# First expert's products in 128-token tiles, wider-spaced transposes, and routing constants spread over attention

## The chip, the core and the metric

The kernel runs on one core of a Trainium2 chip. The metric is device time in microseconds (us). It was run three times: 687.61, 686.19 and 683.44 us, median 686.19 us. One further execution was taken with the profiler; it lasted 685.43 us by the same clock, and its span from the first to the last instruction is 683.8 us. All times "at" some moment below are counted from the start of that span.

## What is computed

Sliding-window attention over 8 batches, 8 heads, 576 positions and 64 values a head; its output, seen as 4608 tokens of 512 values, goes through a mixture of 8 experts with a fixed capacity of 576 tokens each.

```python
def _attn_ref(q, k, v):
    scores = matmul(q, k.T) / sqrt(D)
    # a row sees itself and the 63 rows before it
    attn = softmax(where(mask, scores, -1e9))
    return matmul(attn, v)

def _moe_ref(x, w_gate, w1, w2):
    flat = (x @ w_gate).flatten()
    for idx in argsort(-flat):          # the best pairs first
        tok, e = idx // E, idx % E
        if assigned[tok] >= 0 or counts[e] >= N // E: continue
        assigned[tok] = e; counts[e] += 1
    for e in range(E):
        out[assigned == e] = relu(x[assigned == e] @ w1[e]) @ w2[e]
```

Everything is float32. The products of the experts are made exact enough by splitting each operand into a high part in a rounded 32-bit format (names ending in `h`) and a remainder (names ending in `l`), and adding three products: high by high, low by high and high by low.

## The kernel before

**Attention** (`attention`) runs 72 steps, one for 128 query rows and four heads. A step issues the score matmuls (L126), the softmax on VectorE (L135) and ScalarE (L145), the transposes of the weights (L152, evacuated at L154) and the products with V (L173). Nine steps make one batch. Twice in a batch, the gate's logits are computed too (L85 to L112). At the end of every step from the fifth on, three entries of `setup` are issued: this is the generator `Routing.constants`, 64 small operations, three of them on GpSimd and the rest on VectorE, that build tables the routing needs later. Three a step use it up by step 25.

**Routing** (`Routing.steps`) finds, for one expert at a time, the tokens of highest logit, by eight rounds of a 16-way search. Each round compares all logits with 15 thresholds on VectorE (L461), counts with small matmuls (L518 for the first expert, L532 after it) and picks the next digit. It ends with the list of the expert's 576 tokens (`idx`, L692). The routing of expert 0 has nothing beside it; that of every later expert lies beside the products of the expert before.

**Experts** (`Experts`). For each expert:
- `load` fetches eight chunks of weights (four of `w1`, four of `w2`) and splits them: high part by ScalarE (L790), remainder by VectorE (L794, the first three chunks of expert 0) or by ScalarE and an adding transfer from GpSimd's queue (L799, L801). For expert 0, chunks 3 to 7 start only once `turned` says that all transposes are issued.
- `turn` gathers the tokens with five indirect transfers (L844), 128 tokens each and 64 in the last. It transposes each tile on TensorE (L856) into a buffer `tp`, of which there are two, and splits it: `xh` by ScalarE (L832), then `xl` by VectorE (L835).
- `steps` makes the first products (L897): for each of eight blocks `f` of the hidden layer one unit of 12 matmuls over tokens 0 to 255 and one over tokens 256 to 575. The order begins with three units of the first kind. Each unit is evacuated by ScalarE (`hh`, L874) and VectorE (`hl`, L879). Then come the second products: the last 64 tokens (L929), then four tiles of 128 tokens (L939), each 24 matmuls of 512 columns.

**The order on each engine is written by a planner.** `Streams` runs the Python generators by a clock of its own: each generator issues instructions and says how long they should take (`busy`, `yield`), and the generator whose time comes next issues next. The engines then execute in that order, each in its own queue, and wait for the data they need. So a planned time does not delay anything by itself: it decides what stands ahead of what. `GATHER` is the planner's guess of how long the gathered rows take, and `there` the planned moment at which the last tile has come; tile `a` is planned 1040 ns times (4 - a) ahead of it, and never closer than about 900 ns to the tile before. The first 256-column units may be issued when `XT` is set, after the second tile; those of 320 columns when all five tiles are there (`turned`).

```python
there = self.clock() + self.busy(5200, "pool") + GATHER[min(p, 2)]
yield lambda: self.first == p
...
yield max(0, there - 1040 * (4 - a) - self.clock())
...
yield dt + 600
```

The routing of expert 1 is planned from `turned` of expert 0 on, too.

Of the kernel before, what the change touches and what calls it, by code (L numbers as in the profile page):

```python
# [9 lines left out]
FT = mybir.dt.float32  # L10
# [4 lines left out]
AF = mybir.ActivationFunctionType  # L15
# [7 lines left out]
E = 8  # L23
# [7 lines left out]
def attention(ctx, tc, c, q, k, v, vt, gate, xs, L, choices, setup, counters):  # L31

    nc = tc.nc
# [190 lines left out]
    n = len(seq)  # L224
# [17 lines left out]
    last = []  # L242

    def store(m, x):
        nc.sync.dma_start(xs[128 * m:128 * m + 128], x.rearrange("p h d -> p (h d)"))

    for s in range(n + 4):
        old = seq[s - 4] if 4 <= s else None
        if s < n:
            qk(*seq[s], old)  # L250
        else:
            rs, inv, gates, values = norm(*old)

            for f in (rs, inv, values, gates) if s < n + 2 else (rs, inv, gates):
                f()
            if s >= n + 2:
                last.append(values)
            while late:
                late.pop(0)()
        if 1 <= s < n + 1:  # L260
            sm(*seq[s - 1])

        if stores and (len(stores) > HOLD or s > LOADED):
            store(*stores.pop(0))
        if 2 <= s < n + 2:
            tr(*seq[s - 2])
        if 3 <= s < n + 3:
            pv(*seq[s - 3])
        for f, a in at.get(s, []):
            f(*a)  # L270
        if late:
            late.pop(0)()
        if s > 3:
            for _ in range(3):
                next(setup, None)
    for f in last:
        f()
# [61 lines left out]
CAP = NT // E  # L339
# [390 lines left out]
NCH = 4  # L730
NX = DM // 128
NF = F // 128
LAG = 1500
STAGE = 6

GATHER = (2600, 3800, 6200)
SEND = 3400
LOAD = 2600
ADDED = 4500
# [2 lines left out]
class Experts:  # L742
    def __init__(self, ctx, tc, c, xs, w1, w2, out, ring=8):
        self.tc, self.nc, self.c = tc, tc.nc, c
        self.xs, self.w1, self.w2, self.out = xs, w1, w2, out
        self.ring = ring
        self.fw = ctx.enter_context(tc.tile_pool(name="fw", bufs=1))
        self.ps = ctx.enter_context(tc.tile_pool(name="fp", bufs=1, space=PSUM))
        self.W = {}
        self.XT = {}  # L750
        self.used = 0
        self.taken = 0
        self.first = 0
        self.gathered = 0
        self.sent = 0
        self.turned = 0

    def room(self):
        return self.ps.tile([128, 320], FT, name="h", bufs=3)
# [64 lines left out]
    def turn(self, p, idx):  # L824

        nc, fw = self.nc, self.fw
        yield lambda: self.turned == p

        def evac(a, n, t):
            r = slice(128 * a, 128 * a + n)  # L830
            t = t.bitcast(FT)
            nc.scalar.activation(xh[:, :, r], t[:, :, :n], AF.Copy)  # L832
            yield 700
            self.busy(600, "dve")
            nc.vector.tensor_tensor(xl[:, :, r], t[:, :, :n], xh[:, :, r].bitcast(FT), OP.subtract)  # L835

        def half():
            self.XT[p] = (xh, xl)
            yield 0

        g = fw.tile([128, 5, DM], FT, name="xg")
        for a in range(5):
            n = 128 if a < 4 else 64
            nc.gpsimd.indirect_dma_start(out=g[0:n, a], out_offset=None, in_=self.xs,  # L844
                                         in_offset=IndirectOffsetOnAxis(ap=idx[0:n, a:a + 1], axis=0))
        self.gathered += 1
        there = self.clock() + self.busy(5200, "pool") + GATHER[min(p, 2)]
        yield lambda: self.first == p
        xh = fw.tile([128, NX, CAP], FR, name="xh")
        xl = fw.tile([128, NX, CAP], FR, name="xl")  # L850
        for a in range(5):
            n = 128 if a < 4 else 64
            yield max(0, there - 1040 * (4 - a) - self.clock())
            t = self.ps.tile([128, NX, 128], FR, name="tp", bufs=2)
            for cc in range(NX):
                nc.tensor.transpose(t[:, cc, :n], g[0:n, a, 128 * cc:128 * cc + 128].bitcast(FR), self.c["identr"][0:n, 0:n])  # L856
            dt = self.busy(300)
            self.spawn(evac(a, n, t), dt + 150)
            yield dt + 600
            if a == 1:  # L860
                self.spawn(half(), 600)
        yield 1500
        self.turned += 1

    def steps(self, p, idx):
        nc, fw = self.nc, self.fw
        xh, xl = self.XT[p]

        hh = fw.tile([128, NF, CAP + 64], FR, name="hh")
        hl = fw.tile([128, NF, 512], FR, name="hl")  # L870

        def evac(f, n, h):
            w = h.shape[1]
            nc.scalar.activation(hh[:, f, 256 * n:256 * n + w], h, AF.Relu)  # L874
            yield 500
            for c, m, t in ((0, 256, hl[:, f, 256 * n:256 * n + 256]), (256, 64, hh[:, f, CAP:])):
                if c < w:
                    self.busy(m + 79, "dve")
                    nc.vector.scalar_tensor_tensor(t, h[:, c:c + m], 0.0,  # L879
                                                   hh[:, f, 256 * n + c:256 * n + c + m].bitcast(FT),  # L880
                                                   op0=OP.max, op1=OP.subtract)

        order = [(f, n) for f in range(NF) for n in range(2)]

        order[:6] = [(f, n) for n in range(2) for f in range(3)]
        for f, n in order:
            yield lambda: (p, f // 2) in self.W
            if n:
                yield lambda: self.turned > p
            wh, wl = self.W[p, f // 2]  # L890
            r = (slice(0, 256), slice(256, CAP))[n]
            h = self.room()[:, 0:r.stop - r.start]
            k = 0
            for wt, xt in ((wh, xh), (wl, xh), (wh, xl)):
                wv = wt.rearrange("p (c f) -> p c f", c=NX)
                for cc in range(NX):
                    nc.tensor.matmul(h, wv[:, cc, 128 * (f % 2):128 * (f % 2) + 128], xt[:, cc, r],  # L897
                                     start=(k == 0), stop=(k == 11))
                    k += 1
                    if k % 3 == 0:  # L900
                        yield self.busy((360, 441)[n])
            self.spawn(evac(f, n, h), 100)
            if f % 2 and n:
                self.spawn(self.free(1), LAG)
        self.first += 1

        def put(a, o):
            ot = fw.tile([128, DM], FT, name="ot", bufs=3)
            m = 128 if a < 4 else 64
            if a < 4:  # L910
                nc.scalar.activation(ot, o, AF.Copy)  # L911
            else:
                t = fw.tile([64, DM], FT, name="low")
                nc.scalar.activation(t, o[64:128], AF.Copy)
                yield 650
                self.busy(600, "dve")
                nc.vector.tensor_tensor(ot[0:64], o[0:64], t, OP.add)
            yield max(600, self.sent + SEND - self.clock())
            nc.gpsimd.indirect_dma_start(out=self.out,  # L919
                                         out_offset=IndirectOffsetOnAxis(ap=idx[0:m, a:a + 1], axis=0),  # L920
                                         in_=ot[0:m], in_offset=None)
            self.sent = self.clock() + self.busy(1040, "pool")


        o = self.ps.tile([128, DM], FT, name="o", bufs=2)
        for f in range(NF):
            yield lambda: (p, NCH + f // 2) in self.W
            for n, w in enumerate(self.W[p, NCH + f // 2]):
                nc.tensor.matmul(o, hh[:, f, 512:], w[:, 512 * (f % 2):512 * (f % 2) + 512],  # L929
                                 start=(f == 0 and n == 0), stop=(f == NF - 1 and n == 1))  # L930
                yield self.busy(228)
        self.spawn(put(4, o), 100)
        for a in range(4):
            o = self.ps.tile([128, DM], FT, name="o", bufs=2)
            k = 0
            for f in range(NF):
                wh, wl = self.W[p, NCH + f // 2]
                for wt, ht in ((wh, hh), (wl, hh), (wh, hl)):
                    nc.tensor.matmul(o, ht[:, f, 128 * a:128 * a + 128], wt[:, 512 * (f % 2):512 * (f % 2) + 512],  # L939
                                     start=(k == 0), stop=(k == 23))  # L940
                    k += 1
                    yield self.busy(228)
            self.spawn(put(a, o), 100)
        self.spawn(self.free(NCH), LAG)
# [95 lines left out]
```

## Time and profile before

| quantity | value |
|---|---|
| median of three runs | 686.19 us |
| profiled execution, its own time | 685.43 us |
| profiled execution, span | 683.8 us |
| mean granted clock of TensorE | 0.969 |
| attention, last evacuation of a transpose | 165.66 us |
| list of expert 0's tokens (L692) | 193.41 us |
| first product of expert 0 (L897) | 201.58 us |
| second products of expert 0 (L929) | 235.06 us |
| first product of expert 1 | 274.31 us |
| first product of expert 7 | 625.39 us |

The profile gives, for each instruction, its engine, line, output and inputs, start and duration. A duration of a matmul is modelled and overlaps the next one, so the pace of a group is the distance between starts. A wait "[1.66 <-DMA xg]" in front of an instruction is the time its engine sat idle before it and what ended that time. "PEclk" is the clock granted to TensorE, as a share of the full one.

### The profile page before, as it was taken

How to read it: one execution, taken by the hardware profiler on the slowest of the kernel's cores; microseconds unless marked ns; L12 is line 12 of the kernel's file. 1: busy time of each engine (PE TensorE's matmuls, PEld its weight loads, DVE VectorE, ACT ScalarE, POOL GpSimd, SP SyncE). 2: the span in 40 equal slices, each digit the busy share in tenths (PEclk: the TensorE clock that was granted, in tenths of full speed). 3: DMA queues.
4: the chain of work that ended last, by engine and by line, in shares of the span. 5: the costliest groups of instructions: out<-in, count | busy, mean ns of one | idle time of the engine just before them, and what ended most of it. 6: DMA issues, size and time to landing. Idle time of an engine off the chain costs nothing. (4 is left out here: it accounts for less than half of the span.)

```text
span 683.8 us, 16913 instructions
## 1 busy us (share of the span) xinstructions
PE 639.7 (94%) x6365; PEld 537.0 (79%) x6365; DVE 454.6 (66%) x2262; ACT 360.5 (53%) x733; POOL 176.3 (26%) x203
## 2 busy tenths in 40 slices
PE   7799999998469998999999999999999999999995
PEld 5566777776449875997897799789779889978984
DVE  5999988988776765895896787687778611220300
ACT  4688888886035435627437165444607715634410
POOL 1321222220041115207125132321512433112011
PEclk9999999999559999999999999999999999999998
DMA  8999978921066549829678767938937993962501
GB/s 291 337 361 369 365 279 307 385 97 69 13 202 150 114 145 260 200 47 307 173 140 285 177 149 251 226 83 224 240 123 156 295 266 104 249 163 75 97 24 46
DMA packets 49682, 134.09 MB, mean 196 GB/s; under 512 B 4672, under 2 KB 10432, under 8 KB 49600
## 3 DMA queue, kind: packets, MB, share of 16 engines
q0 software_dynamic: 15552, 54.01, 34.9%
q1 hardware_dynamic: 34048, 79.00, 32.6%
q8 instruction: 50, 0.82, 0.5%
q14 instruction: 32, 0.26, 0.1%
HBM read 82.13 MB, written 18.87 MB: 148 GB/s over the span
## 5 line engine op out<-in xcount | busy, mean ns | idle before, releaser
L879 DVE SCALAR_TENSOR_TENSOR hl<-h,hh 128x256 fp32r<-128x256 f32 x128 | 53.6, 419 | 94.7 <-ACT hh L874 93.8
L939 PE MATMUL o<-wh,hh 128*128 128x512 f32 x256 | 102.6, 401 | 0.0
L939 PE MATMUL o<-wl,hh 128*128 128x512 f32 x256 | 102.3, 399 | 0.0
L939 PE MATMUL o<-wh,hl 128*128 128x512 f32 x256 | 101.4, 396 | 0.0
L145 ACT ACTIVATE pe<-st,mx 128x128 f32<-128x128 f32 x288 | 91.4, 390 | 10.2 <-DVE mx L135 9.0
L874 ACT ACTIVATE hh<-h 128x256 fp32r<-128x256 f32 (+1 forms) x128 | 52.2, 408 | 83.3 <-PE h L897 82.0
L897 PE MATMUL h<-xh,wh 128*128 128x256 f32 (+1 forms) x512 | 94.2, 303 | 0.0
L897 PE MATMUL h<-xh,wl 128*128 128x256 f32 (+1 forms) x512 | 93.4, 301 | 0.0
L897 PE MATMUL h<-xl,wh 128*128 128x256 f32 (+1 forms) x512 | 91.5, 299 | 0.0
L919 POOL DMA_INDIRECT out<-ot,idx x40 | 41.1, 1028 | 191.6 <-ACT ot L911 48.8
L135 DVE CUSTOM_DVE_ANT_0 st<-Sp,mask 128x128 f32<-128x128 f32 x288 | 78.6, 277 | 15.6 <-PE Sp L126 11.5
L911 ACT ACTIVATE ot<-o 128x512 f32<-128x512 f32 x32 | 19.1, 598 | 127.8 <-PE o L939 122.6
L897 PEld LDWEIGHTS h<-xh,wh 128*128 128x128 f32 x512 | 77.2, 192 | 1.1 <-issue 0.4
L897 PEld LDWEIGHTS h<-xh,wl 128*128 128x128 f32 x512 | 76.6, 192 | 0.1
L897 PEld LDWEIGHTS h<-xl,wh 128*128 128x128 f32 x512 | 76.1, 191 | 0.1
L801 POOL DMA_DIRECT2D wl<-st x61 | 55.2, 1063 | 74.5 <-ACT wl L799 53.6
L844 POOL DMA_INDIRECT xg<-xs,idx x40 | 39.8, 995 | 119.6 <-DMA st<-w 40.6
L790 ACT ACTIVATE wh<-st 128x1024 fp32r<-128x1024 f32 x64 | 67.2, 1051 | 6.4 <-DMA st<-w 6.4
L799 ACT ACTIVATE wl<-wh 128x1024 fp32r<-128x1024 f32 x61 | 64.4, 1056 | 0.5
L939 PEld LDWEIGHTS o<-wh,hh 128*128 128x128 f32 x256 | 48.5, 189 | 9.3
L939 PEld LDWEIGHTS o<-wh,hl 128*128 128x128 f32 x256 | 48.4, 189 | 9.1
L939 PEld LDWEIGHTS o<-wl,hh 128*128 128x128 f32 x256 | 48.6, 190 | 8.7
(175 smaller groups left out, 1137.8 us busy)
## 6 DMA issues: line engine op xcount, KB each, us to landing
wl<-st POOLq DMA_DIRECT2D x61, 512.0 KB, 6.8
st<-w SPq DMA_DIRECT2D x59, 512.0 KB, 7.5
xs<-x SPq DMA_DIRECT2D x36, 256.0 KB, 4.8
VO<-v SPq DMA_DIRECT2D x6, 1168.0 KB, 16.0
VT<-vt SPq DMA_DIRECT2D x6, 1152.0 KB, 10.5
Q<-q SPq DMA_DIRECT2D x6, 1152.0 KB, 12.9
K<-k SPq DMA_DIRECT2D x6, 1152.0 KB, 14.4
st<-w POOLq DMA_DIRECT2D x5, 512.0 KB, 6.0
```

The source lines that it names most:

```text
L135: nc.vector.tensor_tensor_reduce(st[:, h, :], Sp[h % 2][:, h // 2], mk, scale=-0.125, scalar=3.0e38, op0=OP.add, op1=OP.min, accum_out=mx[ ...
L145: nc.scalar.activation(pe[:, h, :], st[:, h, :], AF.Exp, bias=mx[:, h:h + 1], scale=-1.0)
L790: nc.scalar.activation(hi, st[i], AF.Copy)
L799: nc.scalar.activation(lo, hi.bitcast(FT), AF.Copy, scale=-1.0)
L801: nc.gpsimd.dma_start(lo.bitcast(FT), st[i], accum_op=OP.add)
L844: nc.gpsimd.indirect_dma_start(out=g[0:n, a], out_offset=None, in_=self.xs, in_offset=IndirectOffsetOnAxis(ap=idx[0:n, a:a + 1], axis=0))
L874: nc.scalar.activation(hh[:, f, 256 * n:256 * n + w], h, AF.Relu)
L879: nc.vector.scalar_tensor_tensor(t, h[:, c:c + m], 0.0, hh[:, f, 256 * n + c:256 * n + c + m].bitcast(FT), op0=OP.max, op1=OP.subtract)
L897: nc.tensor.matmul(h, wv[:, cc, 128 * (f % 2):128 * (f % 2) + 128], xt[:, cc, r], start=(k == 0), stop=(k == 11))
L911: nc.scalar.activation(ot, o, AF.Copy)
L919: nc.gpsimd.indirect_dma_start(out=self.out, out_offset=IndirectOffsetOnAxis(ap=idx[0:m, a:a + 1], axis=0), in_=ot[0:m], in_offset=None)
L939: nc.tensor.matmul(o, ht[:, f, 128 * a:128 * a + 128], wt[:, 512 * (f % 2):512 * (f % 2) + 512], start=(k == 0), stop=(k == 23))
```

## The change

There are four edits.
1. Attention issues three of the routing's constants a step only up to step 9, and one a step from step 10 on. The 64 entries then last to step 55.
2. In `turn`, the planned length of the five gathers is 6400 ns in place of 5200, `GATHER` is 2900 for expert 0 and 6500 for the others (before: 2600, 3800 for expert 1, 6200 for the rest), the planned distance of tiles is 1280 ns in place of 1040, and after a tile's transposes the generator waits `dt + 1000` in place of `dt + 600` for experts 1 to 7.
3. Readiness of tokens is counted by tile (`tiles`). The products of expert 0 may begin after the first tile, those of the others after the second as before; a unit waits for the tiles it reads.
4. Expert 0's units become: six blocks `f` over tokens 0 to 127, six over 128 to 255, six over 256 to 575, and then blocks 6 and 7 as before. That is 12 units of 128 columns in place of 6 of 256. The other experts keep their units and order. A chunk of weights is released after its last unit, which for expert 0 comes later than before for the early chunks.

```diff
         if s > 3:
-            for _ in range(3):
+            for _ in range(3 if s < 10 else 1):
                 next(setup, None)
...
-GATHER = (2600, 3800, 6200)
+GATHER = (2900, 6500)
...
+        self.tiles = [0] * E
...
             nc.vector.tensor_tensor(xl[:, :, r], t[:, :, :n], xh[:, :, r].bitcast(FT), OP.subtract)
-
-        def half():
-            self.XT[p] = (xh, xl)
-            yield 0
+            self.tiles[p] = a + 1
+            if a == (1 if p else 0):
+                self.XT[p] = (xh, xl)
...
-        there = self.clock() + self.busy(5200, "pool") + GATHER[min(p, 2)]
+        there = self.clock() + self.busy(6400, "pool") + GATHER[p > 0]
...
-            yield max(0, there - 1040 * (4 - a) - self.clock())
+            yield max(0, there - 1280 * (4 - a) - self.clock())
...
-            yield dt + 600
-            if a == 1:
-                self.spawn(half(), 600)
+            yield dt + (1000 if p else 600)
...
-        def evac(f, n, h):
-            w = h.shape[1]
-            nc.scalar.activation(hh[:, f, 256 * n:256 * n + w], h, AF.Relu)
+        def evac(f, c0, h):
+            c1 = c0 + h.shape[1]
+            nc.scalar.activation(hh[:, f, c0:c1], h, AF.Relu)
             yield 500
...
-        order = [(f, n) for f in range(NF) for n in range(2)]
-
-        order[:6] = [(f, n) for n in range(2) for f in range(3)]
-        for f, n in order:
+        if p:
+
+            units = [(f, n) for n in range(2) for f in range(3)] + [(f, n) for f in range(3, NF) for n in range(2)]
+            units = [(f, 256 * n, (256, CAP)[n]) for f, n in units]
+        else:
+
+            units = [(f, *r) for r in ((0, 128), (128, 256), (256, CAP)) for f in range(6)]
+            units += [(f, *r) for f in range(6, NF) for r in ((0, 256), (256, CAP))]
+        last = [max(n for n, u in enumerate(units) if u[0] // 2 == i) for i in range(NCH)]
+        for n, (f, c0, c1) in enumerate(units):
             yield lambda: (p, f // 2) in self.W
-            if n:
-                yield lambda: self.turned > p
+            yield lambda: self.tiles[p] * 128 >= c1
...
-                        yield self.busy((360, 441)[n])
-            self.spawn(evac(f, n, h), 100)
-            if f % 2 and n:
+                        yield self.busy(3 * (13.5 + (c1 - c0) / 2.4))
+            self.spawn(evac(f, c0, h), 100)
+            if n in last:
                 self.spawn(self.free(1), LAG)
```

More of the change, by code (lines that the diff above doesn't have):

```diff
@@ L870, in steps @@
         hl = fw.tile([128, NF, 512], FR, name="hl")
-        def evac(f, n, h):
-            w = h.shape[1]
-            nc.scalar.activation(hh[:, f, 256 * n:256 * n + w], h, AF.Relu)
+        def evac(f, c0, h):
+            c1 = c0 + h.shape[1]
+            nc.scalar.activation(hh[:, f, c0:c1], h, AF.Relu)
             yield 500
[L876 to L880, printed above, removed]
-                                                   op0=OP.max, op1=OP.subtract)
-        order = [(f, n) for f in range(NF) for n in range(2)]
-        order[:6] = [(f, n) for n in range(2) for f in range(3)]
-        for f, n in order:
+            for a, b, t in ((c0, min(c1, 512), hl[:, f, c0:min(c1, 512)]), (512, c1, hh[:, f, CAP:])):
+                if a < b:
+                    self.busy(b - a + 79, "dve")
+                    nc.vector.scalar_tensor_tensor(t, h[:, a - c0:b - c0], 0.0, hh[:, f, a:b].bitcast(FT),
+                                                   op0=OP.max, op1=OP.subtract)
+        if p:
[6 more added lines that the diff above has]
+        for n, (f, c0, c1) in enumerate(units):
             yield lambda: (p, f // 2) in self.W
-            if n:
-                yield lambda: self.turned > p
+            yield lambda: self.tiles[p] * 128 >= c1
             wh, wl = self.W[p, f // 2]
-            r = (slice(0, 256), slice(256, CAP))[n]
-            h = self.room()[:, 0:r.stop - r.start]
+            h = self.room()[:, 0:c1 - c0]
             k = 0
@@ L896, in steps @@
                 for cc in range(NX):
-                    nc.tensor.matmul(h, wv[:, cc, 128 * (f % 2):128 * (f % 2) + 128], xt[:, cc, r],
+                    nc.tensor.matmul(h, wv[:, cc, 128 * (f % 2):128 * (f % 2) + 128], xt[:, cc, c0:c1],
                                      start=(k == 0), stop=(k == 11))
```

## The prediction

> **What bounds the kernel now.** I read the page's shares and slices first, then who TensorE waited for, then the engines' busy time in short stretches, then TensorE's own instructions in order of time.
>
> ```profile
> PE 639.7 (94%) x6365; PEld 537.0 (79%) x6365; DVE 454.6 (66%) x2262; ACT 360.5 (53%) x733; POOL 176.3 (26%) x203
> ...
> PEclk9999999999559999999999999999999999999998
> ...
> L897 PEld LDWEIGHTS h<-xh,wh 128*128 128x128 f32 x512 | 77.2, 192 | 1.1 <-issue 0.4
> ```
>
> Read the share of PE in the first line, and the fives of PEclk: TensorE is busy 94% of the span, and only in slices 11 and 12 (171 to 205 us), where expert 0 is routed, is its clock about half. From there to the end its products follow one another, so what counts is each stretch in which it stands still or is slowed. From 197 us on its waits are these (total us, times, longest):
>
> ```profile
> PE tp L856 <- DVE xl L835: 5.3, 8, 1.0
> PE tp L856 <- DMA xg<-xs,idx: 4.4, 4, 1.7
> ```
>
> So 9.7 us of waits stand in front of transposes: 4.4 for gathered rows, 5.3 for a `tp` buffer whose `xl` VectorE had not yet written. The waits also cost clock. These stretches are 3.41 us long, cut where the granted clock changes (columns: length; busy time of PE, PEld, DVE, ACT and POOL; clock; DMA share, GB/s):
>
> ```profile
> 193.87:197.28 3.41, 3.41 (x15) 1.83 (x13) 2.48 (x4) 2.94 (x3) 2.18 (x3) 0.50 0.53 183
> 197.28:200.69 3.41, 1.09 (x9) 0.78 (x8) 3.31 (x8) 1.19 (x2) 2.80 (x3) 1.00 0.71 173
> 200.69:204.11 3.42, 3.05 (x17) 2.99 (x18) 2.21 (x6) 0.78 (x3) 1.91 (x4) 0.50 0.77 214
> 204.11:207.52 3.41, 3.41 (x18) 3.12 (x18) 1.54 (x3) 1.19 (x3) 0.00 (x0) 0.50 0.90 341
> 207.52:210.93 3.41, 3.41 (x28) 3.41 (x28) 2.13 (x6) 2.51 (x4) 0.00 (x0) 1.00 0.04 14
> ...
> 265.54:268.95 3.41, 1.84 (x12) 1.33 (x13) 2.36 (x5) 2.58 (x6) 1.21 (x2) 1.00 1.03 193
> 268.95:272.37 3.42, 3.42 (x16) 2.52 (x17) 2.02 (x8) 0.38 (x1) 0.69 (x1) 0.50 1.11 165
> ```
>
> A stretch with PE busy 1.09 or 1.84 us is followed by one at 0.50, a full one (193.87, 204.11) by one at 1.00; the 3.05 of 200.69 was not enough. Eight of that stretch's 17 records are the transposes of two tiles, and 8 or 9 are products: at half clock some 0.22 us each (twice the 0.120 found below, less their fixed part), 1.8 in all. In 204.11, 4 of 18 are transposes, and the products fill some 2.6 us. So between 1.8 and 2.6 us of products in a stretch raise the clock. From 197 to 300 us three stretches run at half.
>
> **First expert.** All transposes (ns of one: least, median, most), and TensorE at the junction:
>
> ```profile
> L856 PE MATMUL tp<-identr,xg x160: 222/247/339, 198.0 to 602.7; 128*128 128x128 f32 x128, 64*128 64x64 f32 x32
> ...
> 198.01 0.53 PE L856 MATMUL tp<-identr,xg 128*128 128x128 f32 x4 [0.70 <-DMA xg<-xs,idx]
> ...
> 201.58 0.97 PE L897 MATMUL h<-xh,wh 128*128 128x256 f32 x3
> ...
> 209.07 0.64 PE L897 MATMUL h<-xl,wh 128*128 128x256 f32 x4
> 209.55 0.75 PE L897 MATMUL h<-xh,wh 128*128 128x320 f32 x4
> 210.14 0.75 PE L897 MATMUL h<-xh,wl 128*128 128x320 f32 x4
> ```
>
> Starts four matmuls apart give the pace at full clock: (209.55 - 209.07)/4 = 0.120 us for 256 columns, (210.14 - 209.55)/4 = 0.147 for 320.
>
> *Price of narrow units.* 12 units of 128 columns replace 6 of 256: 144 matmuls for 72. No product of 128 columns is in the trace. The line through 256 and 320 columns gives 0.067 us. The nearest rows are the transposes, 128 columns with a new stationary tile each: the group at 263.01 below takes 0.46 for four, less one median duration of 0.25, over three: 0.071. The group at 198.01, which came to an idle engine, gives 0.094. I take 0.071, since products come one behind another: 144 x 0.071 = 10.2 against 72 x 0.120 = 8.6, +1.6 us (ends +1.0 and +4.9). The evacuations double in number beside TensorE; in the rows above DVE is busy 1.5 to 2.2 and ACT 0.8 to 2.5 of 3.41 us, so they are hidden, and would cost their own time if not.
>
> The Trainium skill, "TensorE: Matmul & The Clock Gate", section "Back-to-back issue gap", puts a stream of weight load and matmul at about 81 ns for 128 columns; by it the sum would be 144 x 0.081 - 8.6 = +3.1 us in place of +1.6. The transposes' 0.071 speaks for less.
>
> *Earlier start.* Tile 0's first products need only its `xh`, so TensorE has work from about 199.6 on, between transposes, in place of 201.58 (198.01 + 0.53, and an estimated 1 us for ScalarE's copy and the second tile, which comes 1.5 us behind the first). By 204.1 some 33 narrow matmuls are done (11 ahead of 200.69, then 3.4 less 1.0 for two tiles' transposes, at 0.11 each: 22), worth 16 wide ones, where 8 wide were: 8 x 0.120 = 1.0 us won. The stretch 200.69 to 204.11 then holds 2.4 us of products in place of 1.8, nearer to the 2.6 that raised the clock. So I take it to rise one stretch earlier: half of the 2.9 us of products there, 1.45 won (ends 0 and 3.1, if the clock never falls). Sum: +1.6 - 1.0 - 1.45 = -0.9.
>
> The Trainium skill, "TensorE: Matmul & The Clock Gate", section "Part 4: PE-mode transpose", says that transposes do not count as activity for the clock in the same way; the row at 200.69 agrees.
>
> *What is late next.* Chunks 3 to 7 wait for `turned`, which the planner now puts 1.5 us later (there: 6400 + 2900 for 5200 + 2600). The last chunk already was just in time:
>
> ```profile
> 235.91 0.85 POOL L801 DMA_DIRECT2D wl<-st  x1 [5.12 <-ACT wl L799]
> ...
> wl<-st POOLq DMA_DIRECT2D x1, 512.0 KB, 4.5
> ...
> 240.24 0.42 PE L532 MATMUL rps<-G,one 128*32 128x60 bf16 x9 [1.12 <-DVE q L599]
> 240.58 0.51 PE L929 MATMUL o<-wl,hh 128*128 128x512 f32 x1
> ```
>
> Issued at 235.91, it landed at 240.4, and the second products went on at 240.58; the wait named as VectorE's is in part this one. ACT splits that chunk behind the evacuations of the first products, so it moves with them, but the planner leaves TensorE 1.5 us less of other work before it. Of the 0.9 won I give 0.6 back: first expert **-0.3** (ends -3.0 and +4.5). The routing of expert 1, planned from `turned`, stands 1.5 us later in the queues of TensorE and VectorE; nobody waits for it but expert 1's gathers. On SP's and POOL's queues nothing is passed: the gathers, loads and adds keep their order.
>
> **Expert 1's transposes.**
>
> ```profile
> 261.88 0.53 PE L856 MATMUL tp<-identr,xg 128*128 128x128 f32 x4 [1.66 <-DMA xg<-xs,idx]
> 263.01 0.46 PE L856 MATMUL tp<-identr,xg 128*128 128x128 f32 x4
> ...
> 266.49 0.54 PE L856 MATMUL tp<-identr,xg 128*128 128x128 f32 x4 [0.96 <-DVE xl L835]
> 268.41 0.50 PE L856 MATMUL tp<-identr,xg 64*128 64x64 f32 x4 [0.62 <-DVE xl L835]
> 274.31 0.64 PE L897 MATMUL h<-xh,wh 128*128 128x256 f32 x4
> ```
>
> TensorE stood from 260.22 on (261.88 less 1.66) until the rows came. The first tile was planned 9000 - 4 x 1040 = 4840 ns after the list; now it is 12900 - 4 x 1280 = 7780, that is 2.9 us or 12 matmuls of L939 later: it meets TensorE at about 263, after the rows. Distances grow from 1.04 to 1.3 or more, which covers waits of 0.96 and 0.62. Idle won: 1.66 + 0.96 + 0.62 = 3.2; and a denser stretch 265.54 should not drop the clock, which saves half of 3.4 = 1.7. Together 4.9; I keep 0.4 of waits, **-4.5** (ends -4.9 and -1.5). The tiles now end at the end of expert 0's second products, about 268.5; expert 1's first units need two tiles, written by some 266.5 to 267, and three units of 12 x 0.120 = 1.4 us cover the last three tiles. Were that cover gone, TensorE would wait for `xl`, some 2 us per tile.
>
> **Experts 2 to 7.** Of the 5.3 us for `xl`, 5.3 - 1.58 = 3.7 lie here, six waits of some 0.6. A pair of tiles now lies about 0.35 x 2 = 0.7 further apart, so most vanish: **-3.0** (ends -3.7 and -1.0). The work itself is unchanged and hides under the second products.
>
> **Attention.** Steps 18 to 22 (edges are the evacuations at L154) beside the same five steps of a later batch, then the gate's steps with three constants in each of the first two, beside the same without:
>
> ```profile
> 51.62:60.89 9.27, 8.18 (x151) 6.13 (x153) 9.08 (x67) 7.35 (x21) 3.35 (x5) 1.00 1.05 357
> 111.72:119.30 7.58, 7.58 (x145) 5.70 (x141) 6.56 (x56) 7.02 (x22) 3.37 (x5) 1.00 1.01 379
> 64.62:74.13 9.51, 9.51 (x169) 6.53 (x169) 9.20 (x66) 7.64 (x22) 1.39 (x2) 1.00 1.01 356
> 104.27:113.75 9.48, 9.48 (x169) 6.50 (x169) 8.86 (x61) 7.64 (x22) 1.76 (x3) 1.00 0.71 232
> ```
>
> In the first pair VectorE is the bound (9.08 of 9.27) and the steps are 1.69 us longer; two thirds of the constants leave: about -1.2. In the second pair constants cost 0.03, so one more a step to step 55 is hidden by VectorE's slack. **-1.2** (ends -1.9 and +1.0; DMA, at 1.05, may hold part back).
>
> **Sum.** -0.3 - 4.5 - 3.0 - 1.2 = -9.0. Against the profiled execution's own 685.43 (span 683.8 and 1.6 around it) that is 676.4; the median of the runs is 0.8 above it, so **677 us**.
>
> **Rivals.**
> 1. *Waits move rather than vanish.* ACT and DVE evacuate tiles behind other work, as the 0.96 us at 266.49 shows; later places can collide anew. With half of 4.5 + 3.0 kept, 677 + 3.75 + 1 = 682. The fixed distances speak against it, the planner's ignorance for it.
> 2. *The junction gains nothing.* The clock stays at 0.50 to 207.52 and narrow matmuls take 0.094: 677 + 1.45 + 3.3 = 682.
> 3. *Constants on the path.* If the gate's steps have no slack for them, 46 x 0.15 us come in place of -1.2: 677 + 8 = 685. The 0.03 speaks against it.
> 4. *Slower: narrow matmuls wait for their weights.* Weight loads show 192 ns on the page. Were they not hidden, 144 x (0.192 - 0.071) = +17: 694. It decides from 0.135 us a matmul on (144 x 0.064 = 9.2, the whole gain). Against it: 256 columns run at 0.120 with the same 192 ns, so loads do overlap.
>
> The Trainium skill, "TensorE: Matmul & The Clock Gate", section "LDWEIGHTS (loading the stationary operand)", gives about 107 ns for 128 columns; laid end to end with the matmul this would be some 12 us more, 689; the pace of 0.120 disagrees.
>
> **How the numbers follow.** Forecast 0.60, first rival 0.20, second 0.09, third 0.05, fourth 0.06. The three middle ones stay within 1% of 686.2 (679.3 to 693.1, about what a measurement can tell from no change) but for a little of the first: faster 0.62, same 0.32, slower 0.06. The low end takes the far ends of three gains (-3.7, -4.9, -1.9) and a junction at -3, 673, less 2 for scatter: 671. The high end reaches past the rivals of 682 to the third: 685.
>
> **What would show it.** First product near 199.5 and twelve units of about 0.85 us; clock 1.00 from about 204; no wait above 0.5 us before L856; none at 0.50 after 260; steps 18 to 22 near 8 us. Wrong would be: narrow paces above 0.09, a longer wait for the last chunk, first products of expert 1 waiting for tiles.

## The result: slower by 2.6%, and the profile after

The changed kernel takes 702.49 us (median of 6 runs, 701.35 to 705.57) against 685.38 us for the kernel before (6 runs, 682.85 to 687.61). The ratio is 1.0257, with a 95% interval from 1.0224 to 1.029. The profiled execution took 701.35 us, its span is 699.7 us. The time of 677 us was missed, and so was the range. In experiment 5 below, two of ten executions were slow (702.84 and 706.73 us, mean clock 0.950 and 0.939; the other eight 0.965 to 0.974, the changed kernel's own 0.940 to 0.951) and are left out of its figures.

From the page of the changed kernel, the shares and the granted clock in 40 slices:

```profile
PE 659.1 (94%) x6437; PEld 558.6 (80%) x6437; DVE 452.0 (65%) x2268; ACT 362.9 (52%) x739; POOL 177.4 (25%) x203
...
PEclk9999999998555799999999999999999999999998
```

TensorE has 72 matmuls more than before and 19.4 us more of busy time. There are three fives and a seven (the slices from 175 to 245 us) where two fives stood. Who TensorE waited for, from 150 us on (rows of the same view as in the prediction):

```profile
PE rps L532 <- DVE G L461: 3.3, 2, 2.7
...
PE tp L856 <- DMA xg<-xs,idx: 1.7, 2, 1.5
```

The waits for `xl` are gone, and those for rows are 1.7 in place of 4.4 us. So the change removed the waits it touches, and still the kernel is slower. The moments of each stage show where; a stage's gain or loss is the difference of its two lengths. Each column is one execution.

| moment (us from the start) | before | after | stage that ends here, after less before |
|---|---|---|---|
| end of attention (L154's last) | 165.66 | 164.57 | -1.1 |
| first product of expert 0 | 201.58 | 198.14 | -2.4 |
| second products of expert 0, last 64 tokens | 235.06 | 254.53 | **+22.9** |
| second products, full tiles | 241.39 | 261.72 | +0.9 |
| first product of expert 1 | 274.31 | 288.56 | -6.1 |
| first product of expert 2 | 334.12 | 353.26 | **+4.9** |
| first product of expert 7 | 625.39 | 641.28 | -3.3 |
| end of the span | 683.8 | 699.7 | 0.0 |

The first products of expert 0 take 56.4 us in place of 33.5. TensorE's instructions there, in order of time, in the stretch of narrow units and behind it:

```profile
213.97 1.05 PE L898 MATMUL h<-xh,wh 128*128 128x128 f32 x4
214.82 1.05 PE L898 MATMUL h<-xh,wl 128*128 128x128 f32 x4
215.67 1.05 PE L898 MATMUL h<-xl,wh 128*128 128x128 f32 x4
...
235.94 0.74 PE L898 MATMUL h<-xh,wh 128*128 128x320 f32 x4
236.52 0.75 PE L898 MATMUL h<-xh,wl 128*128 128x320 f32 x4
```

Starts four apart: (214.82 - 213.97)/4 = 0.213 us for a matmul of 128 columns, where 0.071 was forecast, and 0.145 for one of 320. The same part in three stretches (columns as in the prediction; the third figure from the right is the clock):

```profile
198.14:232.58 34.44, 34.24 (x171) 33.67 (x171) 10.55 (x30) 7.57 (x19) 5.34 (x8) 0.50 0.35 98
232.58:235.36 2.78, 2.78 (x12) 2.45 (x10) 1.14 (x6) 1.82 (x2) 0.63 (x1) 0.50 0.00 0
235.36:254.53 19.17, 19.17 (x152) 17.46 (x153) 14.05 (x63) 8.57 (x14) 2.50 (x4) 1.00 0.54 111
```

For 34 us TensorE is busy but for 0.2 us, and its clock stays at 0.50. With the first units of 320 columns it is back at 1.00 after 2.8 us.

### The profile page after: what moved, and what is told of

It reads as the page before. It is cut to its first block, busy times and chain, and to the rows that moved or that the text cites. A ratio compares the mean times of both kernels' runs of the same rounds, so it can differ in the third digit from the quotient of the medians.

```text
span 699.7 us, 17068 instructions
## 1 busy us (share of the span) xinstructions
PE 659.1 (94%) x6437; PEld 558.6 (80%) x6437; DVE 452.0 (65%) x2268; ACT 362.9 (52%) x739; POOL 177.4 (25%) x203
## 5 line engine op out<-in xcount | busy, mean ns | idle before, releaser
L877 DVE SCALAR_TENSOR_TENSOR hl<-h,hh 128x256 fp32r<-128x256 f32 (+1 forms) x134 | 54.5, 407 | 113.3 <-ACT hh L872 112.9
L872 ACT ACTIVATE hh<-h 128x320 fp32r<-128x320 f32 (+2 forms) x134 | 53.3, 398 | 99.4 <-PE h L898 96.9
L898 PE MATMUL h<-xh,wh 128*128 128x320 f32 (+2 forms) x536 | 103.7, 314 | 0.7 <-ACT xh L833 0.7
L898 PE MATMUL h<-xl,wh 128*128 128x320 f32 (+2 forms) x536 | 102.0, 311 | 0.0
L898 PE MATMUL h<-xh,wl 128*128 128x320 f32 (+2 forms) x536 | 101.4, 312 | 0.0
L898 PEld LDWEIGHTS h<-xh,wh 128*128 128x128 f32 x536 | 85.6, 204 | 1.9 <-ACT xh L833 0.8
L898 PEld LDWEIGHTS h<-xh,wl 128*128 128x128 f32 x536 | 85.3, 205 | 0.1
L898 PEld LDWEIGHTS h<-xl,wh 128*128 128x128 f32 x536 | 85.0, 204 | 0.2
L844 POOL DMA_INDIRECT xg<-xs,idx x40 | 41.4, 1034 | 113.1 <-DVE eq L699 61.8
```

What stands on the lines that cost most here:

```text
L872: nc.scalar.activation(hh[:, f, c0:c1], h, AF.Relu)
L877: nc.vector.scalar_tensor_tensor(t, h[:, a - c0:b - c0], 0.0, hh[:, f, a:b].bitcast(FT), op0=OP.max, op1=OP.subtract)
```

## Experiments

Theory N was that the narrow units cost the time; rival S that the later transposes, or the order around them, do.

**1. The change with wide units.** Expert 0's units as before, the rest as changed:

```diff
-            if a == (1 if p else 0):
+            if a == 1:
...
-        if p:
...
-        else:
...
-            units = [(f, *r) for r in ((0, 128), (128, 256), (256, CAP)) for f in range(6)]
-            units += [(f, *r) for f in range(6, NF) for r in ((0, 256), (256, CAP))]
+        units = [(f, n) for n in range(2) for f in range(3)] + [(f, n) for f in range(3, NF) for n in range(2)]
+        units = [(f, 256 * n, (256, CAP)[n]) for f, n in units]
```

> The changed kernel with expert 0's units as before (six of 256 columns where the change has twelve of 128), all else as changed. Theory N (the narrow units cost the time: 144 matmuls at 0.213 us where 72 took 0.120 to 0.213): the first products of expert 0 take 33 to 34 us in place of 56.4, and the kernel 679 to 681 us. Rival S (the later transposes or the order around expert 0 cost the time, and the narrow units only stretch under them): the first products stay above 45 us and the kernel above 690.

It took 682.45 us against 685.08 (ratio 0.9961, 0.9943 to 0.998), and its first products 33.2 us (200.52 to 233.75). Theory N holds; the total is 1.5 us above its band. What else was changed is worth some 2.6 us of the 9 forecast.

**2. The narrow units alone**, in the kernel before:

```diff
-            for _ in range(3 if s < 10 else 1):
+            for _ in range(3):
...
-GATHER = (2900, 6500)
+GATHER = (2600, 3800, 6200)
...
-            yield dt + (1000 if p else 600)
+            yield dt + 600
```

The planned 5200 and 1040 ns were put back too.

> The kernel before with the narrow units and the count of tiles alone; constants three a step, planned times and distances as before. Theory N: first products of expert 0 take 55 us or more, the kernel 705 to 709 us, slower than the full change by what its other parts won (some 4 us). Rival S: below 692.

706.52 us against 685.08 (ratio 1.0327, 1.0276 to 1.0379), first products 56.0 us. The narrow units alone cost some 21 us, and the other edits win 4 of them back in the full change.

**3. What a width costs at full clock.** The kernel of experiment 1 with other widths in late experts:

```diff
+        W256 = ((0, 256), (256, CAP))
+        cut = {2: ((0, 192), (192, 384), (384, CAP)), 3: ((0, 240), (240, 400), (400, CAP)),
+               4: ((0, 128), (128, 256), (256, CAP))}.get(p, W256)
+        units = [(f, *r) for r in cut for f in range(3)] + [(f, *r) for f in range(3, NF) for r in cut]
+        if p == 6:
+            units = [(f, *r) for r in ((0, 128), (128, 256), (256, CAP)) for f in range(6)]
+            units += [(f, *r) for f in range(6, NF) for r in W256]
```

> Expert 0 as before; in later experts, reached at full clock, the units are cut to other widths: 192 in expert 2, 240, 160 and 176 in expert 3, 128, 128 and 320 in expert 4, and in expert 6 the twelve narrow units of the change in its order. What a matmul costs while the clock stands at 1.00: floor theory (a matmul takes at least the array cycles of 256 columns): 0.107 to 0.120 us for every width from 128 to 240. Theory of two cycles a column below 256: 0.107 at 128, 0.133 at 160, 0.147 at 176, 0.160 at 192, 0.200 at 240. Fixed cost theory: 0.213 at any clock. Clock-only theory (narrow matmuls are cheap, only the clock was low): 0.067 to 0.071 at 128, and the line 12 ns + 0.42 ns a column. In expert 6 the clock falls to 0.50 within two stretches of 3.4 us if the stream itself is too thin for it, and stays at 1.00 if the low clock in expert 0 came from the waits ahead of it.

Its time is 710.92 us (one execution alone), with 256-column units replaced in four experts. TensorE in order of time, in experts 3 and 6, and two stretches of expert 6:

```profile
402.35 0.61 PE L897 MATMUL h<-xh,wh 128*128 128x240 f32 x4
402.80 0.61 PE L897 MATMUL h<-xh,wl 128*128 128x240 f32 x4
...
404.55 0.61 PE L897 MATMUL h<-xl,wh 128*128 128x160 f32 x4
404.99 0.61 PE L897 MATMUL h<-xh,wh 128*128 128x160 f32 x4
...
592.41 0.61 PE L897 MATMUL h<-xl,wh 128*128 128x128 f32 x4
592.86 0.61 PE L897 MATMUL h<-xh,wh 128*128 128x128 f32 x4
```

```profile
590.23:606.50 16.27, 16.27 (x147) 16.27 (x146) 3.21 (x11) 11.26 (x21) 3.68 (x4) 1.00 0.63 137
606.50:623.27 16.77, 16.77 (x120) 16.77 (x120) 5.03 (x17) 9.55 (x16) 3.44 (x4) 1.00 0.89 211
```

Groups of four start 0.45 us apart at 240, 160 and 128 columns alike: 0.112 us a matmul, and the median over all groups is 0.112 at 128, 160, 176, 192 and 240. The floor theory holds: any width up to 240 takes nearly the 0.120 of 256 columns. The others fall. The floor shows at half clock too: there the products of 256 columns in this trace start 0.213 us apart in the median, as those of 128 do in the changed kernel, and those of 320 columns there 0.267. And in expert 6 the clock stays at 1.00 through 16 us of narrow matmuls: such a stream does not lower a full clock. The 34 us of the changed kernel then say that it does not raise a halved one either.

**4. The clock kept, with wide units.** More dummy matmuls, whose result nobody reads, while the rows come:

```diff
-            self.warm(16)
+            self.warm(28)
...
             self.spawn(evac(a, n, t), dt + 150)
+            if not p and a < 2:
+                self.warm((12, 8)[a])
```

> As the run with wide units, and TensorE is kept at work while expert 0's rows come: 28 in place of 16 dummy matmuls before the first transposes, 12 after the first tile's and 8 after the second's. Clock theory: the clock stays at 1.00 from about 195 us on where the other run has two stretches at 0.50, and the kernel is 2 to 3.5 us faster than it. Rival: the first products wait for rows and their split anyway, so within 1 us of it, or slower by the dummies in front of transposes.

The clock is 1.00 from 196.5 us to the end of the first products, and these take 31.2 us, 2.0 less: that part of the theory holds. (One stretch at half clock follows at 237.45 and one at 281.83, as in experiment 1 at 239.44 and 283.81.) The kernel takes 681.87 us against 682.45, 0.6 less, which cannot be told from none (ratios 0.995, 0.9927 to 0.9973, and 0.9961, 0.9943 to 0.998). So the 2 to 3.5 us that the theory gave for the whole were missed. By the two traces the lead is 1.8 us at expert 1's first product, 1.3 at expert 2's and 0.7 at expert 3's; in expert 1 TensorE's waits for the routing's comparison grow from 3.6 to 4.3 us (experiment 6 follows them up), and what takes back the rest was not looked into.

**5. The clock kept, with narrow units.** The full change, with dummies ahead of the first tile and behind it:

```diff
-            self.warm(16)
+            self.warm(28)
...
             self.spawn(evac(a, n, t), dt + 150)
+            if not p and a < 1:
+                self.warm(8)
```

> The changed kernel with its narrow units, and TensorE kept at work ahead of them: 28 in place of 16 dummy matmuls before the first transposes and 8 after the first tile's. Theory: the narrow stream holds a full clock but does not raise a halved one. Then the clock stays at 1.00, a narrow matmul takes 0.112 us, expert 0's first products take 38 to 42 us in place of 56.4 and the kernel 685 to 690 us. Rival: the stream drops the clock by itself, 0.213 us a matmul, and the kernel stays above 698.

687.71 us (median of eight executions; ratio 1.0034, 1.0009 to 1.0058), against 702.49 for the change. The stretch of its first products, and two groups in it:

```profile
200.55:240.50 39.95, 39.38 (x335) 37.08 (x334) 24.52 (x98) 17.98 (x34) 7.63 (x11) 1.00 0.56 135
```

```profile
209.43 0.61 PE L900 MATMUL h<-xl,wh 128*128 128x128 f32 x4
209.87 0.61 PE L900 MATMUL h<-xh,wh 128*128 128x128 f32 x4
```

0.112 us a matmul at a clock of 1.00, as the theory gave. So the loss has two parts. The floor is 144 x 0.112 - 72 x 0.120 = 7.5 us by the paces; the first products take 39.8 us where those of experiment 4 take 31.2, 8.6 more, and the kernel takes 5.8 us more. The clock is 144 x (0.213 - 0.112) = 14.5 us by the paces; with it kept the first products take 16.6 us less than in the change (39.8 and 56.4), and the kernel 14.8 us less.

**6. A seventh staging buffer**, on the kernel of experiment 4. It is about the new wait in expert 1, which the changed kernel shows at 302.02 (TensorE), and whose cause lies on ScalarE and VectorE:

```profile
302.02 0.59 PE L532 MATMUL rps<-G,one 128*128 128x60 bf16 x9 [2.73 <-DVE G L461]
```

```profile
298.06 1.06 ACT L791 ACTIVATE wh<-st 128x1024 fp32r<-128x1024 f32 x1 [3.08 <-DMA st<-w]
299.15 1.06 ACT L800 ACTIVATE wl<-wh 128x1024 fp32r<-128x1024 f32 x1
300.11 0.42 ACT L872 ACTIVATE hh<-h 128x320 fp32r<-128x320 f32 x1
```

```profile
300.56 0.42 DVE L877 SCALAR_TENSOR_TENSOR hl<-h,hh 128x256 fp32r<-128x256 f32 x1 [3.28 <-ACT hh L872]
...
301.49 0.79 DVE L461 TENSOR_TENSOR G<-m,thr 128x300 bf16<-128x300 f32 x2
```

Read upwards: TensorE waits for the routing's comparison, this stands on VectorE behind the split of a product, this waits for ScalarE's evacuation, and ScalarE stands before the split of a weight chunk whose transfer has not landed. A stretch at half clock follows (303.63 to 307.04).

```diff
-STAGE = 6
+STAGE = 7
```

> The run with wide units and the clock kept, with seven staging buffers for weights in place of six. Theory: the new wait of TensorE in expert 1's first products (3.8 us, then a stretch at half clock) comes from ScalarE, which stands 4.1 us before the split of chunk 6 because its load needs the staging buffer of chunk 0, freed late by the adding transfer. With a seventh buffer that load starts earlier: the wait and the halved clock go, 3 to 5.5 us faster. Rivals: it moves to chunk 7, so 0 to 2 us; or the transfers themselves are the limit, no change.

678.82 us against 681.87, 3.05 less, the lower end of what the theory gave. TensorE's wait for the comparison is 1.5 us in all in place of 4.3, and no stretch at half clock is left between 199 and 673 us.

**7. The old distances for experts 1 to 7**, on the kernel of experiment 4:

```diff
-        there = self.clock() + self.busy(6400, "pool") + GATHER[p > 0]
+        there = self.clock() + self.busy(5200 if p else 6400, "pool") + (GATHER[0], 3800, 6200)[min(p, 2)]
...
-            yield max(0, there - 1280 * (4 - a) - self.clock())
+            yield max(0, there - (1040 if p else 1280) * (4 - a) - self.clock())
...
-            yield dt + (1000 if p else 600)
+            yield dt + 600
```

> The run with wide units and the clock kept, with the planned times and distances of the transposes of experts 1 to 7 as before the change. Theory: the distances are worth what the waits on the buffers were, some 3 us over experts 2 to 7, and at expert 1 next to nothing, since what is won there is lost again to the late weights: 2 to 4 us slower. Rival: the full 4.9 us at expert 1 count too: 6 to 8 us slower.

684.29 us, 2.4 slower (ratio 0.9981, 0.9963 to 0.9998, against 0.995, 0.9927 to 0.9973; the intervals still overlap, and the stages below show it more clearly). The waits before transposes are back, in the same view as above:

```profile
PE tp L856 <- DVE xl L836: 5.4, 8, 1.0
```

By stages, expert 2 begins 1.2 us earlier than in experiment 4 (331.7 and 332.9 us), and expert 7 2.0 us later (623.4 and 621.4): the distances are worth 3.2 us in experts 2 to 6, and up to expert 2 they win nothing; in this pair they lose 1.2.

**8. A longer planned load**, on the kernel of experiment 4. It changes only the order, on ScalarE above all:

```diff
-LOAD = 2600
+LOAD = 4000
```

> The run with wide units and the clock kept, with the planner's time for a weight load at 4000 ns in place of 2600, so that ScalarE's splits stand later in its queue, behind evacuations of products. Theory: the order on ScalarE carries the wait in expert 1; with the split of chunk 6 behind the evacuations, these no longer stand behind a transfer: 2 to 5 us faster. Rival: chunks then come late to the second products, or nothing changes because the split still stands ahead: within 1 us or slower.

676.41 us, 5.5 less (ratio to before 0.9855, 0.9825 to 0.9885): the fastest kernel of the study beside its equal in experiment 10. ScalarE's longest wait for a weight transfer in expert 1 falls from 4.1 to 0.8 us, and no stretch between 245 and 670 us is below full clock. Expert 1 takes 60.0 us, from its first product to that of expert 2, in place of 65.5. So the order carried the wait, on ScalarE where it showed; more room for loads helps too, but only in part.

**9. Both**, on the kernel of experiment 4:

```diff
-LOAD = 2600
+LOAD = 4000
-STAGE = 6
+STAGE = 7
```

> The run with the longer planned load, with seven staging buffers too. Theory: both take away the same wait in expert 1, so together they bring no more than the longer load alone: within 1.2 us of it, 675 to 678 us. Rival: the staging buffers carry a wait of their own in every expert: 2 us or more faster.

680.17 us, in a set of runs where the kernel before took 687.9: the ratio is 0.989 (0.9856 to 0.9924), no better than 0.9855. The rival falls. By ratio it is a little behind, which the theory did not say: the intervals overlap, but its trace has a stretch at half clock, from 538.87 to 542.28 us, that experiment 8 has not, and expert 5 takes 61.3 us there in place of 58.1. Ahead of that stretch TensorE waits 1.46 us, up to 536.79, for the routing on VectorE (L672); why it came late was not followed up.

**10. Expert 0's chunks sooner**, on the kernel of experiment 8:

```diff
-            yield max(100, dt - 1200) if p or i < 3 else 3500
+            yield max(100, dt - 1200) if p or i < 3 else 2300
```

> The run with the longer planned load, with the planned pause between expert 0's weight chunks at 2300 ns in place of 3500, so that its last chunk is split some 5 us earlier. Theory: the second products of expert 0 wait for that chunk (their first part takes 8 us for 12 matmuls of 0.23 us and the routing between them, and a stretch at half clock follows); with it early 3 to 5 us faster. Rival: the wait is that of the routing's counts on VectorE, which stand in TensorE's queue there, or the splits now hold up evacuations: within 1 us or slower.

678.34 us, ratio 0.9866 (0.9831 to 0.9901): no gain over 0.9855 that can be told, where the theory gave 3 to 5 us. Yet its place is right: the last 64 tokens of expert 0 take 4.7 us (233.13 to 237.78) in place of 8.1, and expert 1 begins 3.7 us earlier (265.54 and 269.25). By expert 7 the two kernels are level (616.85 and 616.93); the 3.7 us are given back in small sums, 1.4 in expert 1 and 1.6 in expert 5 the largest.

## Why the prediction was wrong, and where it was right

- **Price of narrow units: wrong, and it decided.** The step took 0.071 us from the transposes, and with it the first expert came to -0.3 us; its three stages measured -2.4 + 22.9 + 0.9 = +21.4. The runs show 0.112 us a matmul at full clock and 0.213 at half, beyond the 0.09 that the prediction named as a sign of being wrong. The error was to carry a price from one kind of instruction to another because their widths agree. The profile of before held a sign that the two kinds differ. All weight loads of the transposes (ns: least, median, most):

```profile
L856 PEld LDWEIGHTS tp<-identr,xg x160: 134/139/224, 198.0 to 602.7; 128*128 128x128 f32 x128, 64*128 64x128 f32 x32
```

  They last 139 ns in the median, those of the products 192 in the mean. Rival 4 had the mechanism nearly right and got a chance of 0.06: not that a load comes on top of the matmul, but that a matmul below 256 columns takes no less time than about 256 do. By floor alone, 0.112 lies under the 0.135 from which that rival was to decide.
- The Trainium skill, "TensorE: Matmul & The Clock Gate", section "LDWEIGHTS (loading the stationary operand)", gives about 107 ns for a load of 128 columns. I laid it end to end with the matmul and dismissed it (and the 12 us I gave for it do not come out of its figure: 144 x 0.107 is 15.4). As a floor beside the matmul it fits 0.112 within 5 ns. That the load is the cause was not shown: no run takes the loads away. A least length of a product near that of 256 columns fits as well, and at half clock 128 and 256 columns do take the same 0.213; no run tells the two apart.
- **Clock up one stretch earlier: wrong.** The prediction read from two rows that between 1.8 and 2.6 us of products in a stretch raise the clock, and counted narrow products like wide ones. The narrow stream was busy for 34.24 of 34.44 us and the clock stayed at 0.50, in ten stretches of 3.41 us on end. What the clock goes by instead stays open. By the paces this turned 7.5 us into 22.
- **Earlier start: right in its moment, wrong in its worth.** The first product comes at 198.14 (forecast near 199.5), 2.4 us earlier after attention's 1.1 is taken off. But by 204.1 TensorE had begun 21 narrow matmuls where 33 were forecast, so the 1.0 us of work won was not there: what began earlier ran slower.
- **Late next, the last chunk: right in kind**, 0.9 us longer where 0.6 was given back (1.8 longer with wide units, in experiment 1). Experiment 10, which starts the chunks sooner, takes 3.4 off that stage.
- **Expert 1: half right.** The waits before its transposes went, and no stretch lost its clock there: 6.1 us were won up to its first product, more than the far end of 4.9. Then 4.9 us were lost in it, to a wait that was not foreseen: the weights of its second half, for whose transfers the kernel before had those 6 us more. The net is -1.2 in place of -4.5. The prediction asked whether expert 1's tiles would be there, not whether its weights would, and did not look at ScalarE's queue, where a late chunk holds up the evacuations.
- **Experts 2 to 7: right**, -3.3 for -3.0 up to expert 7's first product, and experiment 7 gives 3.2 for experts 2 to 6. The stretch takes 288.0 to 288.6 us in the traces of the change and of experiments 1, 4 and 6, and 291.3 and 291.7 before and in experiment 7; where one more stretch ran at half clock, it takes 290.7 (experiment 5) and 294.0 (experiment 2, with the old distances).
- **Attention: right where it was read, not shown for the whole.** Steps 18 to 22 were forecast near 8 us. They take 7.8 to 8.1 in all ten traces with the thinned constants, and 9.3 and 9.0 in the two with three a step (before and experiment 2). But the end of attention lies anywhere from 164.2 to 166.2 us in those ten traces, and at 165.7 and 165.3 in the two, so that the table's -1.1 meets the forecast -1.2 is in part luck.

Without the narrow units, the change is 2.6 us faster, within 1% (experiment 1); with the dummy matmuls and the planner's time for loads set anew as well, 9 us (experiment 8).

## What to carry to other kernels

A price belongs to an operation, its type and its width together; where no row has all three, the bound must reach to the price of the next width that the trace does have, here 0.120 us for 256 columns, by which the narrow units alone would have taken 144 x 0.120 - 8.6 = 8.6 of the 9 us forecast. Here a clock that had fallen was not raised by matmuls of 128 columns, and keeping TensorE at work through the wait ahead of them won 14.8 us; ahead of wide ones the same won nothing that can be told. So look at what follows a wait: wide matmuls first, or no wait. And a stall removed in a planned order uncovers the next late input: look, on every in-order queue, for the instruction that waits for a transfer and for what stands behind it.

## What the runs showed of the hardware

- Products of a stationary tile of 128 x 128 in the rounded 32-bit format take 0.112 us at full clock for 128, 160, 176, 192 and 240 columns, 0.120 for 256 and 0.147 for 320 (experiments 3 and 5). At half clock 128 and 256 columns both take 0.213, and 320 take 0.267. Transposes of 128 columns, in the group at 263.01 of the kernel before, start 0.06 to 0.08 us apart.
- The granted clock has a memory. With 128-column products it stayed at 0.50 for 34 us in the changed kernel and at 1.00 for 19 us in that of experiment 5, and for 16 us in expert 6 of experiment 3. The first two run the same products in the same order; the dummies ahead of them and behind the first tile are all that differs. The Trainium skill, "TensorE: Matmul & The Clock Gate", section "What's actually happening", lets a busy stretch of some 3.4 us release the clock; with wide products the traces agree (a stretch with 2.8 us of 320 columns sufficed), with narrow ones they do not.
